# Attention and maxout feed-forward on one core: another written order of instructions and another list of masked tiles

## The chip, the cores and the metric

The kernel runs on one core of a Trainium2 chip. The core has a matrix engine (PE, with the loading of weights shown apart as PEld), a vector engine (DVE), a scalar engine (ACT), a general engine (POOL), and SP, which here only issues transfers to the 16 DMA engines. Every engine works through its own instructions in order and waits for others by semaphores. The metric is the device time of one execution in microseconds (us). Smaller is better.

## The reference

```python
scores = (1 / sqrt(64)) * q @ k.T                    # q, k, v: batch 8, heads 8, 576 rows, 64 columns
thresh = max(scores, axis=-1) - tau                  # tau = 0.02
scores = where(scores >= thresh, scores, -1e9)
attn = softmax(scores)                               # the sum gets + 1e-9
x = (attn @ v), heads side by side                   # 4608 x 512
h = maximum(maximum(x @ w1, x @ w2), x @ w3)         # 4608 x 768
out = h @ w_out                                      # 4608 x 512
```

The keep-or-drop decision is made against the row's largest score, so scores and softmax are done in 32-bit floats; the attention weights, v, x, h and the matrices of the feed-forward part are bf16.

## The kernel before

**Pieces.** The work is cut into pieces that the function `issue` emits one at a time. A *quad* is four heads of one batch (16 quads). A quad has 9 *chunks* of 128 query rows (four of head pair 0, one with the 64 rows that are left of each pair, four of pair 1). In a chunk each partition holds rows of two heads, so that a chunk has two *halves* (r = 0, 1), each a tile of 128 x 576 scores. Chunks run in the order of batches and quads; batch 7 alone (`SPLIT`) is cut into two parts, of 256 and of 320 rows.

**The order is written out by hand.** `ORDER` is one string of letters, and a loop at the end of the kernel calls `issue` on each. A letter takes the next piece of its kind, so the string sets only how the kinds interleave. Instructions of one engine keep the order of the string (`_Ordered` ties each to the one before it); between engines only data and buffers order them. The digit behind S, T, O, F is one of four PSUM slots (`bank`), and a slot must have been read out before the next piece takes it. All instructions of the pieces are recorded in `_Ordered.run`, line 90 of the kernel, so the profile tells them apart by tile, not by line.

| letter | engine | piece (tile in the profile) |
|---|---|---|
| S | PE | scores of one half (sc) |
| T | PE | transposes of q or k of a quad (tp); four per quad: q and k of r = 0, then of r = 1 |
| O | PE | attention weights times v (o), four per batch, four for each part of batch 7 |
| F, B | PE | first and second part of a feed-forward piece (ph: 18 per batch; po: the output). The 576-row pieces of ph and the po of two column blocks have both, the others F alone. The po of the last 64 rows of a batch ("ninth") is written among the pieces of the next |
| m | DVE | row maximum of a half, from PSUM; for a masked half it also writes the negated scores to z |
| e | ACT | masked: exp of z. Not masked: a Prelu with a very small negative slope, from PSUM to z |
| k | DVE | masked: drops what is below the threshold and sums (z<-z, SCALAR_TENSOR_TENSOR) |
| n | ACT | not masked: exp with the sum (z<-z, ACTIVATE and a read of the accumulator) |
| r | DVE | reciprocal of both sums of a chunk |
| p | POOL | multiplies one half by its reciprocal and writes bf16 (P), two per chunk |
| t | SP | DMA that transposes a chunk's P into ptq |
| a, c | ACT, DVE | q and k out of PSUM (qt, kt) |
| q | POOL | the other half of the partitions of q (qs) |
| x, w | ACT, DVE | x out of PSUM (xt) |
| h, v, u | ACT, DVE, ACT | ph to hm; the two maxima (hm, hT); po to the output tile (ob, obr) |
| l, g, o | SP | loads of q, k, v of a quad (eight: q's rest, k's rest, q, k, two of v, two of v's rest); load of a block of weights (stage, 512 KB, two buffers); store |
| y, z | POOL | cast of v (three per quad: vb, two of vr), of a block of weights (w, wo) |

An S of a half needs the quad's qt, qs and kt. An O needs nine t of its quad (four or five in batch 7's parts) and the y of it. The first F of a batch needs all four x or w of the batch, and the F of a block of weights its z. A g needs the z of two blocks before it.

**Two ways to the same half.** `MASKED` has one digit for each half, 288 in all, in the order of the S. A half with 1 goes m, e, k and costs DVE a pass over SBUF; its PSUM slot is free after m. A half with 0 goes m, e, n and costs ACT a second pass; its slot is free after e. Both give the same numbers up to rounding.

**In front of the string** (the prologue) the first quad is loaded, transposed and copied out, with some matmuls to warm PE up (`WARM`, `FILL`).

Of the kernel before, what the change touches and what calls it, by code (L numbers as in the profile page):

```python
# [21 lines left out]
FLAT = 2.0 ** -100  # L22

MASKED = """
101000100110000110011100001010010001100010001000101000010000100000100010
000011110101100001001001001001000001011100101011000110001010010000010011
001010011101100000101100100001001010000110011111000001000100000110000101
001001001101100000110001000100101000001100010011100101110110000001111111
"""


# [5 lines left out]
PBUFS = 6  # L37

ORDER = """
glllllS0lylS1mylyeS2zmlkS3lelmnlT0mS1aS2rmeqS0meqmeS3pnkT1pT0nrcaptemS0yeS1mgS2eympeS3mqtnT1S0mqnS2knrceprmS  # L40
1epkepeS3mnyS0rkptemnS2pmnlzmS3erremtpT0empS1eklpaS2kgnS0ptnmeprrmlS1epS3mleS2pmlS0eplmetpmeS1knS3tkernkS2pt
nmnprmtepmS1eqS0melpmT2ntrmT3pnrcpatekS3pekS2eqnrS1mtnqmS0pemepS3tmeqS2kepT1lnrcnprtmS0nT1pmS3epmgS2atpmeO1k
yermeO0knptrerT3wpnT2cS1aptmnS3pS2xmptS1emzS0emeS3zgmeS2lrmpnS0lmO1eplmeplknO3qlnrwleplkS1xqgS2ertmF3npF0meT
1pBrteBkyhS2cpnS3mpS1nvF2npmF0eqBmeqBrrvepS3tkhT2pS1nmS0lapmetS2pmeS3mzeF0mF1ezgBrnF2vpgnBktByeF0rvhpS3ntS2p
mF1npmBeBqrveT3zncT0F2taqvS3nBpmnS0tprhS1rmpeS3mtpS2emeyS0mteF1zmeF3kBelqBnvgF2pngT0vBnqlrS1cphS3lrmnS0plmO2
eplmeptS1ewpS3nmF0znmS2lBezkgO3etymyS1vegkF0ntF2nrrmpBxBpveS3phS0mtnF1prmeBprS2evptS3nmF0pnS1mplBermS3ztnS2v
nzS1meS0tmpeF3mperkS2petBmepmS0tkuF1ukelkT3elBkntrarmpS2uS3pmulS0eymtO1empnrO2kpewS3xpS1elmpF2lmF0eyqBrlkeT3
ytBhcF1pnT2vT3qlaBclnS0qvlS2nqtF3mnyF1meS0pBemBthrrF2kpeS3vnBpmF0nS1pveBrprS3mhtS2pmeS0pmeS1tpmF2emF3peBtkeT
0BvaF1onvqT2T0tBcqaS3nkqS0lhrmS2nlpmF1elpF3meBlkBelF0vntS2rvnBpS1mhplS3melF0mS2teBrmepS1rkpO3emnqO2tnrvpnwyS
0xlprS3emoF2pmoT1eyBpctS3evyF0nS1mtnS2pmBeympF1hkS3eyF2rekT0ptBamBnpS0veF3qtvS1urmnpS2mF3epketT0nkT1Bnrmparr  # L50
cpS2uS1pumtS0empS3emqoS1eF2mqlemqleS3kplnS0mBlepmlekT1teO3kunktO0urcpnrrwlS2nplS1xmpS3lmpS0eompS1eF2mtpeF3me
BkBetS0khF1nrmF2pnBvpBerrvS3phS0mtnpS1mF2peS3mtpeBmeF1yvF0etByknBvnS2tS3rhmpS1melpS0meF3lmF2elBkeBlvT1ntF0nv
T3BacS2ohS1rrmlpnF3lmF0peoBkpeBovnT2oS1qavS3tnprO2rmpmleqS0wtnT3pS1mepO2mteqkeqF0nS1cxBympnS3rS2hytmS1emF0pe
F3mpeBrkBpetF2vnF1pBnvS0thkS3nmF2BmeBveF0rrvpT1uS3kapS0nmS2F1pmtepmeS3rktepS0mnS2pmlBelrmeplS3kupS0lurmS2elp
F1mnoqmeS0qreS2lmpS3elmBpelmptekO0nketO2ukurrnwpT3T1xpcS0aF2ymyT3tpS1ceBqmS3thqF0meF2pknBtBnvF1nS3rtrvpeBmS0
phS2lmepS1lmyS3etF0meyF2mpeBkBetF1knF3vnBBrvhpS0nvT1pF2nmF3takBeS0rvplBmS1phlrS2remplF3mpleF0klBpeS1lvnS2lpm
nBtrO3mepvnptS2nwS1emF0mF3eBrkepS2hBrmS1nptvS0npT2meO3qmeycqlT0xT1yS2lacF3ntmyT0yeF1kqBatrBrevqF0hkS2pnoS3mF
1pmBteBpveS2qntS0vpnF3mprS1mlueS3pmoS0nqmtF2epmekT1oBerocpetrkS3npS1nmS0lpumS3uopmS1eT2mF0aokeorS3remplS2emt
pS1emBpeklqtkO3uqunO0rtmpewpT2xtS3cpeS0mnF2tF1meBknF3lkBhlBevF2nS0vnBmS1hrrS3pmeF0pmS2eBpmteF1pveF3kBlnS0vnl
S2rrBnmlpS1hrlmpF0eF3mtpeBkpBevtS2nF1pvnT0pBtmaS3hS0metF1rmepT2BrcepS3nvptT0S2nmyS1amS3lepmS0leO2mlelmeO1rkp  # L60
ewnT3pF0xcF2nykBnS1vnBrmS3phF0rrmepS2BynmqF1levF3qlBekpF0onvS2tBqmBhqrS1lepvT2S3lampF0lmS2peoBkpetF1vnS3prmu
S0ntqmS1eF2pmetpmeS3rkepS1tBmnpmelrS0keptS3muS1uymS0temT2yeF3pcntknT2BkelramtpS1nS2pmuS0leqrmO1tuqrkepO3nwep
mS1xpS2metF3pmS0eqBmeF1yhrkT2pBtecF3nS0vpnlS2rmpS1nlmBpnF0lveS2tmF3eBmeBkleF1klhF2lnrBvplS0nrrvptBnS3mphS1my
teS2mF3epmF0eBpeBtvpT1nrS2yvnlS3maF0omnqS1kBepF3temS2hpBrrmeS0ptveS1pmS3nptS2meO0pmeymnqlO3weokeoF1xkT0tT2S3
rcapBnmlF2pnS0vqtBerrmpS1hF3mqeT2BpncF0evptF2nkBpT1nvBlaS3ylS0hmoF1yqmT2eoBqrcnF0tpS3ervT2pBmaF1ytkqS2uvnS3q
mS1epF0mepmeS2kteT3BrnrcponmpS1uryS3umtS2emF0pepomeS1opnS2mtpeO3myektnO1wnkS2xrS3repmS1mpBekpteS2muS3purmF1e
pF0tmeBpkS3ntBhS2rnmpO1empO3xvS2xtnkS1eF3rmpF0emByepBveF1tkS2hS3mBmF0eF2rvepBBpvS1htkO3nmO0xkS2xeS3rmF0pF1me
pBeBtvS2F3vF0mF1kBeBkhF2nrvBpnBrvpS3hS0ptmS1pmeS2mtnF0mF3eBrnpBvnF1pS2vntS0rmpBmF3phoS2eS0omeF1tmBeBkO2vO0rv
pF3kpF1uketeF3kekBwrrkpBukxpuF2F0hptF1vF2pvF0hF1tvF2rvpF0hF1vpF2vF0thF1uvF2uvF0hoF3vF1vF2hoF0voO3oO1wovF2xF3
uoF0F1hF2vF0vF1hF2vF0vF1hF2vF0vF1hF2vF0vF1hF2vF0vF1hF2vBvF0uuooBF1uuuooo  # L70
"""


# [633 lines left out]
```

## Time and profile before

| | |
|---|---|
| median of 3 runs | 451.03 us (449.19 to 451.13) |
| profiled execution | 449.93 us; its span from first to last instruction 448.1 us |
| busy: PE, PEld | 427.0 us, 317.6 us |
| busy: DVE, ACT, POOL | 399.4, 392.4, 314.2 us |
| DMA | 87.44 MB in 212,773 packets, 195 GB/s over the span |
| granted TensorE clock, mean over the span | 0.988 |
| masked halves (k), others (n) | 109, 179 |

How to read it: busy is the time in which an engine worked on at least one instruction. PE's matmuls are pipelined and their ends are modelled, so that a busy PE need not be at its peak. In lines of groups, the number behind the bar is the group's busy time, then the mean time of one instruction in ns, then the idle time of the engine just before them and what ended it. Transfers issued by SP are listed under SPq; SP itself is never counted as busy. The page's 40 slices are 11.2 us each, their digits are tenths.

### The profile page before, as it was taken

How to read it: one execution, taken by the hardware profiler on the slowest of the kernel's cores; microseconds unless marked ns; L12 is line 12 of the kernel's file. 1: busy time of each engine (PE TensorE's matmuls, PEld its weight loads, DVE VectorE, ACT ScalarE, POOL GpSimd, SP SyncE). 2: the span in 40 equal slices, each digit the busy share in tenths (PEclk: the TensorE clock that was granted, in tenths of full speed). 3: DMA queues.
4: the chain of work that ended last, by engine and by line, in shares of the span. 5: the costliest groups of instructions: out<-in, count | busy, mean ns of one | idle time of the engine just before them, and what ended most of it. 6: DMA issues, size and time to landing. Idle time of an engine off the chain costs nothing.

```text
span 448.1 us, 14065 instructions
## 1 busy us (share of the span) xinstructions
PE 427.0 (95%) x5195; PEld 317.6 (71%) x5195; DVE 399.4 (89%) x1101; ACT 392.4 (88%) x793; POOL 314.2 (70%) x417
## 2 busy tenths in 40 slices
PE   7766889999999999999999999999999999999995
PEld 6524647767688768878687867868687787787762
DVE  3799999899999999999999999999999999999641
ACT  3899999999899999999999999999999999866422
POOL 3798889989785985587776785659777787534400
PEclk9898899999999999999999999999999999999999
DMA  8989999999999999999999997999998999546722
GB/s 235 266 195 188 234 238 190 249 244 220 250 192 193 187 236 209 207 215 179 227 175 205 228 217 176 217 230 205 197 195 203 204 156 194 108 78 132 130 95 107
DMA packets 212773, 87.44 MB, mean 195 GB/s; under 512 B 185824, under 2 KB 199648, under 8 KB 212704
## 3 DMA queue, kind: packets, MB, share of 16 engines
q1 hardware_dynamic: 212000, 85.69, 94.6%
q8 instruction: 41, 0.67, 0.6%
q10 hardware_dynamic: 704, 0.85, 0.6%
q14 instruction: 28, 0.23, 0.2%
HBM read 34.60 MB, written 9.44 MB: 98 GB/s over the span
## 4 chain that ended last, share of the span: by engine, by line
PE 77%; DVE 7%; ACT 5%; POOL 3%; DMA 3%; issue 2%; SPq 1%; DVEq 0%; POOLq 0%; ACTq 0%
PE ph L90 30%; PE sc L90 28%; PE po L90 10%; PE o L90 7%; ACT z L90 5%; DVE z L90 4%; PE tp L90 3%; DVE unused L90 2%; POOL P L90 2%; DMA qm<-in_q_dram 1%; DMA km<-in_k_dram 1%; SPq L90 1%; DVE hm L90 1%; DMA out_dram<-ob 1%; DVE kt L90 0%
## 5 line engine op out<-in xcount | busy, mean ns | idle before, releaser
L90 POOL TENSOR_SCALAR P<-z,rs 128x576 bf16<-128x576 f32 x288 | 228.8, 809 | 89.2 <-DVE rs L90 45.2
L90 PE MATMUL sc<-kt,qs 64*128 64x256 f32 (+2 forms) x640 | 180.5, 423 | 7.7 <-DVE z L90 2.0
L90 PE MATMUL sc<-kt,qt 64*128 64x320 f32 (+2 forms) x640 | 181.1, 433 | 4.0 <-DVE kt L90 1.2
L90 PE MATMUL ph<-xt,w 64*128 64x288 bf16 (+2 forms) x2160 | 165.5, 283 | 0.4 <-DVE hT L90 0.2
L90 PEld LDWEIGHTS <-w 64*128 64x128 bf16 (+1 forms) x2160 | 127.3, 94 | 29.8 <-issue 7.2
L90 ACT ACTIVATE z<-sc,nm 128x576 f32<-128x576 f32 x179 | 128.9, 740 | 10.8 <-DVE unused L90 9.5
L90 DVE TENSOR_SCALAR_CACHE_REDUCE unused<-sc 128x576 bf16<-128x576 f32 x179 | 130.5, 751 | 8.2 <-PE sc L90 7.3
L90 ACT ACTIVATE z<-z 128x576 f32<-128x576 f32 x179 | 120.8, 680 | 0.1
L90 PEld LDWEIGHTS sc<-kt,qs 64*128 64x128 f32 (+1 forms) x640 | 92.3, 179 | 30.9 <-ACT z L90 7.8
L90 PEld LDWEIGHTS sc<-kt,qt 64*128 64x128 f32 (+1 forms) x640 | 92.2, 178 | 20.0 <-ACT z L90 5.4
L90 DVE SCALAR_TENSOR_TENSOR z<-z 128x576 f32<-128x576 f32 x109 | 89.1, 832 | 0.2
L90 DVE TENSOR_SCALAR_CACHE_REDUCE z<-sc 128x576 f32<-128x576 f32 x109 | 80.5, 752 | 7.9 <-PE sc L90 4.6
L90 ACT ACTIVATE z<-z,nm 128x576 f32<-128x576 f32 x109 | 81.5, 772 | 2.6 <-DVE z L90 2.0
L90 POOL COPY qs<-qt 64x512 f32<-64x512 f32 (+1 forms) x63 | 45.0, 714 | 15.0 <-ACT qt L90 11.9
L90 PE MATMUL po<-wo,hT 64*128 64x512 bf16 (+1 forms) x480 | 54.0, 356 | 0.1
L90 DVE TENSOR_TENSOR hm<-ph,hm 128x576 bf16<-128x576 f32 (+2 forms) x54 | 37.1, 687 | 11.7 <-PE ph L90 11.3
L90 ACT ACTIVATE hm<-ph 128x576 bf16<-128x576 f32 (+2 forms) x54 | 32.1, 595 | 15.2 <-PE ph L90 13.7
L90 PEld LDWEIGHTS <-hT 64*128 64x128 bf16 (+1 forms) x480 | 29.3, 97 | 17.0 <-issue 3.1
L90 DVE TENSOR_TENSOR hT<-ph,hm 128x576 bf16<-128x576 f32 (+2 forms) x54 | 37.2, 688 | 3.8 <-PE ph L90 0.9
L90 PE MATMUL o<-ptq,vb 128*64 128x512 bf16 (+2 forms) x544 | 38.9, 282 | 0.2
L90 ACT ACTIVATION_READ_ACCUMULATOR z<-z 128x1 f32 x179 | 35.4, 198 | 0.0
L90 PEld LDWEIGHTS <-vb 128*64 128x64 bf16 x544 | 23.5, 111 | 14.4 <-issue 4.4
(33 smaller groups left out, 278.2 us busy)
## 6 DMA issues: line engine op xcount, KB each, us to landing
vm<-in_v_dram SPq DMA_DIRECT2D x32, 256.0 KB, 4.2
out_dram<-ob SPq DMA_DIRECT2D x31, 256.0 KB, 2.8
qm<-in_q_dram SPq DMA_DIRECT2D x15, 512.0 KB, 4.7
km<-in_k_dram SPq DMA_DIRECT2D x15, 512.0 KB, 5.1
stage<-in_moe_w_dram SPq DMA_DIRECT2D x9, 512.0 KB, 4.5
ptq<-P SPq DMA_TRANSPOSE x144, 4.2
stage<-in_moe_w_out_dram SPq DMA_DIRECT2D x3, 512.0 KB, 4.9
qm<-in_q_dram SPq DMA_DIRECT2D x16, 64.0 KB, 2.9
```

Source lines behind the costliest of these rows:

```text
L90: ins = fn(*a, **kw)
```

## The change

`ORDER` and `MASKED` are replaced. The new string is as long as the old (3,312 characters) and has the same number of every letter but two: k 105 instead of 109, n 183 instead of 179, in step with `MASKED`, whose rows have 21, 27, 25 and 32 ones instead of 23, 28, 27 and 31. Of the digits, slot 0 is taken 135 times (141), slot 1 142 (143), slot 2 149 (147), slot 3 144 (139). All engines get their letters in another sequence: the first letters that differ are the 1st of SP, the 3rd of DVE, the 4th of ACT and POOL, and the 10th of PE. The functions that make the pieces, the buffers and the prologue stay.

```diff
@@ -22,10 +22,10 @@
 FLAT = 2.0 ** -100
 
 MASKED = """
-101000100110000110011100001010010001100010001000101000010000100000100010
-000011110101100001001001001001000001011100101011000110001010010000010011
-001010011101100000101100100001001010000110011111000001000100000110000101
-001001001101100000110001000100101000001100010011100101110110000001111111
+001100101001000000011101001010000001100010001000101000011000100000100000
+000011111001100001001001001001000001011100101001000110001010010000010011
+000010011101100001001100100001001010001100010111000001000100000110000101
+001001001101100000110001000100100100001100100011100111010011010111110110
...
@@ -37,37 +37,37 @@
 PBUFS = 6
 
 ORDER = """
-glllllS0lylS1mylyeS2zmlkS3lelmnlT0mS1aS2rmeqS0meqmeS3pnkT1pT0nrcaptemS0yeS1mgS2eympeS3mqtnT1S0mqnS2knrceprmS
-1epkepeS3mnyS0rkptemnS2pmnlzmS3erremtpT0empS1eklpaS2kgnS0ptnmeprrmlS1epS3mleS2pmlS0eplmetpmeS1knS3tkernkS2pt
-nmnprmtepmS1eqS0melpmT2ntrmT3pnrcpatekS3pekS2eqnrS1mtnqmS0pemepS3tmeqS2kepT1lnrcnprtmS0nT1pmS3epmgS2atpmeO1k
-yermeO0knptrerT3wpnT2cS1aptmnS3pS2xmptS1emzS0emeS3zgmeS2lrmpnS0lmO1eplmeplknO3qlnrwleplkS1xqgS2ertmF3npF0meT
-1pBrteBkyhS2cpnS3mpS1nvF2npmF0eqBmeqBrrvepS3tkhT2pS1nmS0lapmetS2pmeS3mzeF0mF1ezgBrnF2vpgnBktByeF0rvhpS3ntS2p
-mF1npmBeBqrveT3zncT0F2taqvS3nBpmnS0tprhS1rmpeS3mtpS2emeyS0mteF1zmeF3kBelqBnvgF2pngT0vBnqlrS1cphS3lrmnS0plmO2
-eplmeptS1ewpS3nmF0znmS2lBezkgO3etymyS1vegkF0ntF2nrrmpBxBpveS3phS0mtnF1prmeBprS2evptS3nmF0pnS1mplBermS3ztnS2v
...
-pF0tmeBpkS3ntBhS2rnmpO1empO3xvS2xtnkS1eF3rmpF0emByepBveF1tkS2hS3mBmF0eF2rvepBBpvS1htkO3nmO0xkS2xeS3rmF0pF1me
-pBeBtvS2F3vF0mF1kBeBkhF2nrvBpnBrvpS3hS0ptmS1pmeS2mtnF0mF3eBrnpBvnF1pS2vntS0rmpBmF3phoS2eS0omeF1tmBeBkO2vO0rv
-pF3kpF1uketeF3kekBwrrkpBukxpuF2F0hptF1vF2pvF0hF1tvF2rvpF0hF1vpF2vF0thF1uvF2uvF0hoF3vF1vF2hoF0voO3oO1wovF2xF3
-uoF0F1hF2vF0vF1hF2vF0vF1hF2vF0vF1hF2vF0vF1hF2vF0vF1hF2vBvF0uuooBF1uuuooo
+lllS0llmlS1yelgS2ymylS3emgnlT0mleS1lakS2nlqermS3ylmeS0pmeS1kpS3elmS2nlzmelrmnT1pS0tcnperkT1pameS1zmteS3knpS0
+rnmpemS2permeqS1mnqT3meqktepS0ncS2ntrpmS3npretprmeS1pmnS0tpmS3npmS1etpmeS0rT2mnplkeT1akgeS2qmgepmteS3rkpeknt
+S0perrnmT2pncS3ptamepS1meqtrS2meyqnS3lmqeS0pmelpknT1lpS2nmeymeS3lrkepS0tcnT2rpnmS1tpnmaprrmS0eS2pmteS1pmT3ep
+ctepmeT3O0ykntnyS2etrykpnO1wnprmaS0xptrS3meS2zmeS1mzgeS0mlnS3pmleS1pmelO2qmelpkteO0nrnklpS3nlwgxprrmS2leS0pm
+eF3qtmT1eBqcF0eqkthBpnS2vS1nF3pmnF0pmBerBkepS2vhT1tnprmS0S3apmetS1zmeS2rmpeF3tmF0epBkepF1tnBvBznvS2ghS3rymnF
+0gmS1eplBrkepF2tnmF3BnpvBnqvT1S0hprrcT2S3pamS1eymzF2emBeqgkF0etyS3nS1vpnmtF2pBmezBveS3prgnS0mtS1phrmT3epO2me
+tzeF0wpnS1gcqS2nmBqnmO3zekepgS1xvlF2nS3mtnF0rrmpBeBlpveS1lphS2mntF3zmeBrpS0evS1lpnmF2lnpS3rmleBptmS1nzvS0nS3
+mtpnS2rpeF1rmepmtepS0mBepmtekF3ektekT2uBarklpukS0uqlS2urS1mlnS3pmleO0pmlepmelO2wtnkS1xrS0tepmF2myF3eBkepT1tB
...
+meF0opmnBtykBhpS1ervS2eptmO3pO0mxnS3txS2rmepF0empF1ekBtBevF3hkS2nS0mnBrmF1npF2vepBkBtS0hvO3emO2xkS1xerS3rpmF
+2mpF0eF1kpteBnBvpF3BvtBrhkpF2S0vS1prmBptmF3eF0pveBtBhS1vS2mS3mF0F1mBkBF2vhF3keBeO0vnO1kF2kxeBwurS1rvpS0mpS2F
+3mpetmpeS0eoF1mnketBknkBurrupoF2puF0hptF3uvF2pvF1hF0tvF3rvpF2hF1vopF0vF3thF2vF1vF0hoF3vF2ovF1hF0vF3vO2uoO1wF
+0xF3F2hF1vF3vF2hF1vF3vF2hF1vF3vF2hF1vF3vF2hF1vF3vF2hF1vBvF3uuooBF2uuuooo
 """
```

More of the change, by code (lines that the diff above doesn't have):

```diff
@@ L45 @@
-mF1npmBeBqrveT3zncT0F2taqvS3nBpmnS0tprhS1rmpeS3mtpS2emeyS0mteF1zmeF3kBelqBnvgF2pngT0vBnqlrS1cphS3lrmnS0plmO2
-eplmeptS1ewpS3nmF0znmS2lBezkgO3etymyS1vegkF0ntF2nrrmpBxBpveS3phS0mtnF1prmeBprS2evptS3nmF0pnS1mplBermS3ztnS2v
-nzS1meS0tmpeF3mperkS2petBmepmS0tkuF1ukelkT3elBkntrarmpS2uS3pmulS0eymtO1empnrO2kpewS3xpS1elmpF2lmF0eyqBrlkeT3
-ytBhcF1pnT2vT3qlaBclnS0qvlS2nqtF3mnyF1meS0pBemBthrrF2kpeS3vnBpmF0nS1pveBrprS3mhtS2pmeS0pmeS1tpmF2emF3peBtkeT
-0BvaF1onvqT2T0tBcqaS3nkqS0lhrmS2nlpmF1elpF3meBlkBelF0vntS2rvnBpS1mhplS3melF0mS2teBrmepS1rkpO3emnqO2tnrvpnwyS
@@ L50 @@
[L50 to L64, printed above, removed]
@@ L65 @@
-rcapBnmlF2pnS0vqtBerrmpS1hF3mqeT2BpncF0evptF2nkBpT1nvBlaS3ylS0hmoF1yqmT2eoBqrcnF0tpS3ervT2pBmaF1ytkqS2uvnS3q
-mS1epF0mepmeS2kteT3BrnrcponmpS1uryS3umtS2emF0pepomeS1opnS2mtpeO3myektnO1wnkS2xrS3repmS1mpBekpteS2muS3purmF1e
-pF0tmeBpkS3ntBhS2rnmpO1empO3xvS2xtnkS1eF3rmpF0emByepBveF1tkS2hS3mBmF0eF2rvepBBpvS1htkO3nmO0xkS2xeS3rmF0pF1me
-pBeBtvS2F3vF0mF1kBeBkhF2nrvBpnBrvpS3hS0ptmS1pmeS2mtnF0mF3eBrnpBvnF1pS2vntS0rmpBmF3phoS2eS0omeF1tmBeBkO2vO0rv
-pF3kpF1uketeF3kekBwrrkpBukxpuF2F0hptF1vF2pvF0hF1tvF2rvpF0hF1vpF2vF0thF1uvF2uvF0hoF3vF1vF2hoF0voO3oO1wovF2xF3
@@ new lines @@
+eF3qtmT1eBqcF0eqkthBpnS2vS1nF3pmnF0pmBerBkepS2vhT1tnprmS0S3apmetS1zmeS2rmpeF3tmF0epBkepF1tnBvBznvS2ghS3rymnF
+0gmS1eplBrkepF2tnmF3BnpvBnqvT1S0hprrcT2S3pamS1eymzF2emBeqgkF0etyS3nS1vpnmtF2pBmezBveS3prgnS0mtS1phrmT3epO2me
+tzeF0wpnS1gcqS2nmBqnmO3zekepgS1xvlF2nS3mtnF0rrmpBeBlpveS1lphS2mntF3zmeBrpS0evS1lpnmF2lnpS3rmleBptmS1nzvS0nS3
+mtpnS2rpeF1rmepmtepS0mBepmtekF3ektekT2uBarklpukS0uqlS2urS1mlnS3pmleO0pmlepmelO2wtnkS1xrS0tepmF2myF3eBkepT1tB
+hcF0nqvT2T1laByrcynS3qvS2nlqmF1tnpF0meS3pBelmBlhrrF2kpelS1vnBlprF3mnlS0pveBtprmS1hS2pmeS3tpmeS0pmF2emF1eBkeT
@@ new lines @@
+3BvatF0nvqT2T3BkqlaS1nrcS3phmtS2npmF0epF1mteBqkBeqF3lnvS2lnBrvplS0hmtpS1F3meS2mteBrmepS0vnpO1rekpnO3mtnpweS2
+yrrtxS1mF0yymT3epBcnS1pvS2nptF3meS0pmeBomT2hS1okeF0omF3ntBkaBervS1ponrF2vpemS0ptuS3mpeF2metknT1T3rknBparrceS
+0puS3mqtuS1mpeS2mpeS3lmF0peomepS1ketqT3S2ncBqnmlqnmlO3ekluktO1urnwperrS0pxS3mptnS2mS1pempS3etmF0peF2meBlkBel
+S1khoF3nrmlF0pnBtvpBerrvS2phlS1mnpS3tmF0peS2mpeBmeF3vF1eoBkntS0vnBS2rmhpS3mepS1mteyF2mF0eyBkteBnrvT3pF1aovT2
+ynBplrcS3hplS0mnyF2lmF1elBykepBlnvT3tS0aS2vnO3rrmtpnmpeS1weptS2mS0prmO3eqtmeqF1eqlT0S2xqcBnlpmS3hlpS0meF2ymF
@@ new lines @@
+1elBknlF3vnBokBetS2hvS0nrrF3mpF1mpeBkBpetF2vnprS0uvnT3ptmS2aS1pmeS0trmF3epmnpkeS2tS0ermpBnmopnkS1uS2rurompS0
+eF3ompelmpeS2lkpeS0lmS1elqBmelqmetkO2unktO0erwpurkpT1txT2cS3apF0nmtT1qS2ceBqmnS1yF3hmF2eyrBpeBvptnF0pS1vnBrm
+tpS3hS2pmeS0mtS1eF3meF2meBkBeF0knF1vnBBrvhpS3nvT0pF2akyF1tnBmyS0velByrmlS3phS2rlempF1lmyeF0pklBepS3tnvS2nBrm
+ptO1meprvepS2wnS3plmF0nF1rmepBlkeqS2lBhmtT3nyS0vnS2mqlO1emtpecT2xT0rS3pacF1eqmF2lnyBklqeT0BvlaS3khoS1qnmF0tF
+2pmeBrBopnvS3teprvF0pnrmS1puS2meS3prmS0epF1tmepmepT2ktBeqncT3tuS0kaS2urqmS3tnpmS1nF0pmemteS3repS1mS2lepmBely
@@ new lines @@
+kteS3kuO1rumplnmlpO0ewterpT2xS1cqnoS3mpF0nF2metBkeBkF1hlF3nvBlnrrS0pvlnBpmS2lhS1ymleF0mtS3epBmepF2vF1etkBnS0
+vnS3rmBnpS2rhmpF0emF1pteBkpBerF3vnS2ptvnT0pBramS1pthS0mepF3meqtT2rBecpS1nvylT0ynS2pmlS3amlS1eomS0elO2rmpeome
+plO3ketnwT1F0nctF2xkBnBrvpS1hrF3pmS0qBemqS2onvF1yeF0mBopkeF3tyBnS2vqhBrlrnmpT1S0vaptS2empF1S3mpelBkeplF0vntS
+2rumS1pnS0mtepF3rmepmetqS2kS0epBnmmteS1rkepS2lmuS0ulpmS1nlymT3yetF2cekeT3oBrknpamoS0npS3mnS1qtmuO0qurrmqelO2
+wpelkpelS0xS3meptF2mS1peBemytF0hrkT3pBecF2nS1vpnS3rymtBpnmS0epS1vlnF3mF2etBmeBkhF0lkeF3nBrvpS1nrvBpnS2mptS0h
@@ new lines @@
+mpeS3meF2tmF1eBkeBlrvnT0plS3ravlpS2nlmqF0nlS1mqeBtrrmpF2eS3phBlmepS0tvepS1mS2npS3mepO0meknO1meownT3orxkT2pS0
+tacF1nF2qrmeBtpS3evpBmS0tyhF1meT2yBcqoeF3rpkT2F0aptBnvBnS2pvS1hqtmF3nqT0meBrS1npvF2npmT3BactS1ervF3prmS0pueS
+2ompF3ekqelmT1ntS0qcnBpmekteS2S1urrmpF0uompekS3eptS2nmS1pnmlO3ermtpekO2pnwS1ykxtyS3emS2BomeyrmepS1rukpS2uoF3
+meF0opmnBtykBhpS1ervS2eptmO3pO0mxnS3txS2rmepF0empF1ekBtBevF3hkS2nS0mnBrmF1npF2vepBkBtS0hvO3emO2xkS1xerS3rpmF
+2mpF0eF1kpteBnBvpF3BvtBrhkpF2S0vS1prmBptmF3eF0pveBtBhS1vS2mS3mF0F1mBkBF2vhF3keBeO0vnO1kF2kxeBwurS1rvpS0mpS2F
```

## The prediction

> **What bounds the kernel now.** I read the page first, then busy time by stretch, then the waits, the timeline of the first 24 us, the chain, and the queue of SP. The profiled execution took 449.93 us: a span of 448.1 and 1.8 around it. The median of three runs is 451.03 (449.19 to 451.13), so the sum is made against 449.93 and then set on 451.03.
>
> The page, busy share and its 40 slices of 11.2 us:
>
> ```profile
> PE 427.0 (95%) x5195; PEld 317.6 (71%) x5195; DVE 399.4 (89%) x1101; ACT 392.4 (88%) x793; POOL 314.2 (70%) x417
> ...
> PE   7766889999999999999999999999999999999995
> ```
>
> PE has holes in its first six slices and nowhere else. By stretch (columns: PE, PEld, DVE, ACT, POOL busy, granted clock, DMA):
>
> ```profile
> 14.00:30.00 16.00, 12.29 (x98) 7.27 (x98) 14.35 (x43) 15.66 (x32) 12.85 (x18) 0.89 0.88 214
> 30.00:45.00 15.00, 10.06 (x86) 5.74 (x86) 14.45 (x46) 14.94 (x32) 13.22 (x17) 0.88 1.13 196
> 45.00:60.00 15.00, 12.77 (x124) 9.56 (x124) 14.56 (x40) 14.43 (x31) 13.77 (x17) 0.89 1.09 224
> 60.00:80.00 20.00, 19.22 (x231) 12.82 (x229) 19.12 (x56) 19.90 (x40) 18.35 (x24) 1.00 1.07 226
> 80.00:97.00 17.00, 16.93 (x219) 12.19 (x215) 16.03 (x42) 16.93 (x37) 16.23 (x22) 1.00 1.14 226
> 97.00:150.00 53.00, 52.86 (x680) 38.72 (x678) 50.16 (x140) 50.12 (x104) 42.00 (x56) 1.00 1.09 218
> 150.00:200.00 50.00, 49.89 (x643) 38.22 (x642) 48.70 (x134) 47.54 (x96) 35.88 (x49) 1.00 1.07 215
> 200.00:300.00 100.00, 99.95 (x1284) 76.54 (x1281) 94.84 (x262) 94.69 (x189) 71.06 (x95) 1.00 1.02 201
> 300.00:400.00 100.00, 100.00 (x1300) 78.48 (x1300) 94.14 (x260) 92.44 (x189) 71.85 (x99) 1.00 0.94 179
> ```
>
> Two regimes. From 14 to 97 ACT is busy 15.66 + 14.94 + 14.43 + 19.90 + 16.93 = 81.9 of 83 us, and PE, which has only scores to make until the first batch's softmax is through, 71.3: ACT sets the pace. From 97 to 400 PE is busy 302.7 of 303; ACT has 2.9 + 2.5 + 5.3 + 7.6 = 18.2 us to spare there. So the end moves by what the first stretch gains or loses and by any new hole in the second. One wait of the first stretch belongs to neither engine. The timeline at 12 to 24 us, and the chain:
>
> ```profile
> 13.43 0.53 PE L90 MATMUL tp<-identf,qm 64*128 64x64 f32 x10 [2.57 <-DMA qm<-in_q_dram]
> ...
> 13.99 0.70 ACT L90 ACTIVATE qt<-tp 128x640 f32<-128x640 f32 x1 [1.70 <-PE tp L90]
> ...
> 14.82 0.76 DVE L90 TENSOR_SCALAR_CACHE_REDUCE unused<-sc 128x576 bf16<-128x576 f32 x1 [1.88 <-PE sc L90]
> ```
>
> ```profile
> 7.90 5.39 DMA qm<-in_q_dram
> ```
>
> The second quad's q, issued at 7.90, lands at 13.29; PE, ACT and DVE all stand for it. What SP had issued before:
>
> ```profile
> 6.20 0.59 SPq L90 DMA_DIRECT2D stage<-in_moe_w_dram  x1
> 6.84 0.51 SPq L90 DMA_DIRECT2D qm<-in_q_dram  x1
> 7.39 0.47 SPq L90 DMA_DIRECT2D km<-in_k_dram  x1
> 7.90 0.47 SPq L90 DMA_DIRECT2D qm<-in_q_dram  x1
> ```
>
> **The change, part by part.** Counted by letter, the two texts hold the same pieces; only k goes from 109 to 105 and n from 179 to 183. Held against the trace, the old text is a time line: of the 2,425 letters of PE, ACT, DVE and POOL that I could lay on instructions, 96% start no more than 0.3 us before any that is written ahead of them. So places in the new text can be compared with places in the old.
>
> *PE's work.* Same letters, and the banks are used about equally often (135 to 149 times each, were 139 to 147): 0. An S takes 0.43 to 0.54 us to the next start, by its neighbour; S followed by S goes from 156 to 151 places, so at most 5 x 0.11 = 0.5 either way.
>
> *The masks.* Four fewer masked tiles: DVE loses four k, ACT gains four n.
>
> ```profile
> L90 ACT ACTIVATE z<-z 128x576 f32<-128x576 f32 x179 | 120.8, 680 | 0.1
> ...
> L90 DVE SCALAR_TENSOR_TENSOR z<-z 128x576 f32<-128x576 f32 x109 | 89.1, 832 | 0.2
> ```
>
> One n is 120.8/179 = 0.67 us, one k 89.1/109 = 0.82: ACT +2.7, DVE -3.3 in all. Behind 97 us the 18.2 us of ACT's room hide it; without that cover it would cost 2.7. In front of it the place decides: before the 75th S (which starts at 103.4 us in the trace) the new text has 49 n instead of 48 and 21 k instead of 23, with all other ACT letters (73 e, 8 a, 3 x, 6 h) and all PE letters equal. ACT paces here, so this costs one n: **+0.7** (bounds 0.7 to 1.3, since before the 59th S it is two n less one h, and before the 88th two n).
>
> *The start of SP's text.* Old: `glllll`; new: `lllllllg`. The 512 KB of `stage` go behind the second quad's q and k. That takes 0.64 us of issue (6.20 to 6.84) from in front of qm, and 0.52 MB from the transfers that it shares the engines with, at 0.32 to 0.38 MB/us (the slices of the DMA view from 8.5 us on) 1.4 to 1.6 us; the two overlap. The weights are not missed: z1 is written 1.5 us of PE work in, now 6.1, and the first F starts near 68 us. Also, ACT's letters ahead of the first a go from `een` to `eene`: 0.65 us of work falls into the 1.70 us hole. The gain on ACT is at least that 0.65 and at most the hole, 1.7. The landing term is nearer to the upper end, since qm then waits for nothing but its own quad: **-1.5**.
>
> *Loads moved.* Before the third quad's load is due nothing changes; for the fourth, q is issued 1.8 us of PE work ahead of its T where it was 4.4 (in ACT's letters 4.0 us, was 9.8). Loads issued near 42 and 50 us took 4.3 to 4.7 us from their place to landing. So PE may stand 0 to 0.7 us there, at about 45 us, while ACT has up to three written-out banks in front of it: 0, or 0.7 if it has none.
>
> *Transposing DMAs and products.* SP issues the 144 transposes in order with loads and stores, and an O waits for nine of them. The smallest rests between the landing and the O in the trace: 0.29 us at the third O (63.6), 0.34 at the seventh (118.2), 0.46 at the thirty-fifth (425.2), 1.6 at the fifth (94.6). In PE work, the last transpose is written ahead of these: third 2.8, now 3.3; thirty-fifth 3.1, now 3.9; fifth 5.8, now 4.3; seventh 6.3, now 5.0. The first two gain. The other two lie where SP runs late:
>
> ```profile
> 79.91 12.49 SPq L90 DMA_TRANSPOSE ptq<-P  x6
> ```
>
> From 79.9 SP issues without a pause, and the 27th transpose, written at 87.6, lands at 93.0: 5.4 us later; the 36th 6.6 us later. In the new text three more of them are out by 80 us (25 instead of 22), so the lag at these two should be some 3 x 1.3 us smaller. Bounds: 0 and 3.2 us (below); I take 0. The Trainium skill, Perfetto Trace Analysis, section What "DMA-bound" means, counts a kernel as DMA-bound where the issuing engine's track is solid with DMA slices; by that rule nothing gained on ACT would reach the end and the sum would be the rival's below, +2.4. The trace so far sides against it: every O found its tiles landed.
>
> *The end.* Four S move behind the thirty-third O, and the work that covers the last x is now the outp half of 1.3 us alone instead of ninth and outp (2.1 us); the last x is 0.43 us, so 1.3 still cover it. The stretch behind the last O is letter for letter the same. 0, bounds -0.3 and +1.0 (a wait for the last transpose).
>
> Sum: -1.5 + 0.7 = **-0.8**: 449.1 in an execution like the profiled one, 450.2 against the median.
>
> **Rivals.** (1) *SP comes late* (slower). Place: the fifth O. Its last transpose is written 4.3 us of PE work ahead (5.2 us at the rate at which 5.8 took 6.9), behind g9, which now waits for z7 (1.04 us), and with one more load (0.65) and one more g (0.5) ahead. If the lag stays 5.4, the tile lands 5.4 + 2.2 = 7.6 behind: PE stands 2.4 to 3.2. The seventh O adds up to 0.7 to 1.6 if the first stop has not let SP catch up. With the gain of 0.8: +1.6 to +3.9, say 454.0. It decides once the lag is over some 5.2 us. For it: SP's solid track, DMA share over 1.0. Against: three transposes moved ahead of 80 us. (2) *The fill gains all* (faster): the hole of 1.7 goes, with DVE 1.6 lighter by the 75th S half of ACT's 1.1 us of idleness goes, and PE's 0.85 us of idleness between 60 and 97 too: -1.7 + 0.7 - 0.6 - 0.85 = -2.5, 448.6. Against: e still waits on m across two engines. (3) *The load is not sooner*: qm is held by its own 512 KB and by k's; then -0.65 + 0.7 to 1.3, 451.0 to 451.7.
>
> **The numbers.** Forecast 0.38, rival 1 0.27, rival 2 0.22, rival 3 0.13. A measurement of this kernel can tell about 0.5% (2.3 us) from no change. Forecast and rival 3 lie within; of rival 2 nearly all passes -2.3 once its bounds are stretched by PE's 0.5; of rival 1 most passes +2.3. Faster 0.24, same 0.49, slower 0.27. The range leaves out the far ends of both: 447.2 to 454.6; the forecast's own is 449.0 to 451.6.
>
> **What would show it.** Right: the first tp<-qm matmul of the second quad starts near 12 us, ACT's gap in front of its qt is under 0.5, PE from 97 on is still busy 99.8%, O never waits on ptq, and ACT is busy some 395 us. Wrong: a PE wait named DMA ptq near 93 or 117 us (rival 1), tp still at 13.4 (rival 3), or PE holes from z or hm behind 100 us, which no row of before has.

## The result, and the profile after

The changed kernel took 446.46 us (median of 5, 446.20 to 447.21), the kernel before 451.03 in the same comparison (449.19 to 452.03): a ratio of 0.9911, interval 0.9883 to 0.9939. A second comparison of the same two gave 447.77 (7 runs, 446.23 to 449.69) and 0.9939, 0.9918 to 0.9961. Over all comparisons below the medians are 447.3 (13 runs) and 450.9 (97 runs): the change is worth 3.6 us, where I forecast 0.8. The profiled execution took 447.21 us with a span of 445.4 (449.93 and 448.1 before), a difference of 2.7. Two of the three kernels below that got idle matmuls also had longer runs at a lower mean clock (0.926 to 0.965), and their times and ratios are of the other runs alone.

The page after: PE has the same 5195 matmuls in 1.5 us less of busy time, although the half clock lasted longer in this fill (13.7 us, 10.2 before); ACT is 1.4 up, DVE 4.3 down.

```profile
PE 425.5 (96%) x5195; PEld 316.4 (71%) x5195; DVE 395.1 (89%) x1093; ACT 393.8 (88%) x801; POOL 314.9 (71%) x417
...
PE   7677799999999999999999999999999999999995
```

By stretch, the same stretches and columns as before (PE, PEld, DVE, ACT, POOL busy, granted clock, DMA share and GB/s):

```profile
14.00:30.00 16.00, 10.53 (x86) 5.94 (x84) 15.59 (x46) 15.38 (x34) 15.27 (x18) 0.88 1.03 244
30.00:45.00 15.00, 11.99 (x87) 9.10 (x88) 13.39 (x40) 14.17 (x29) 12.30 (x17) 0.73 1.10 213
45.00:60.00 15.00, 12.16 (x126) 7.76 (x122) 14.19 (x41) 14.89 (x33) 14.40 (x20) 0.95 1.06 212
...
97.00:150.00 53.00, 52.79 (x688) 39.78 (x684) 49.79 (x141) 50.77 (x104) 42.66 (x55) 1.00 1.12 227
150.00:200.00 50.00, 49.87 (x638) 37.16 (x636) 47.13 (x132) 48.70 (x100) 35.56 (x50) 1.00 0.96 205
200.00:300.00 100.00, 100.00 (x1307) 75.18 (x1305) 94.98 (x262) 96.22 (x196) 70.89 (x98) 1.00 0.98 204
300.00:400.00 100.00, 100.00 (x1286) 77.70 (x1285) 93.49 (x261) 91.51 (x185) 76.03 (x98) 1.00 0.93 181
```

The two regimes are still there. PE is busy 302.7 of 303 us from 97 on, as before, and the busy column alone would say that nothing happened there; the table of stretches below says otherwise. In the fill, the second quad's q, from the timeline and the chain:

```profile
11.55 0.53 PE L90 MATMUL tp<-identf,qm 64*128 64x64 f32 x10 [1.46 <-DMA qm<-in_q_dram]
12.12 0.70 ACT L90 ACTIVATE qt<-tp 128x640 f32<-128x640 f32 x1
...
7.33 4.08 DMA qm<-in_q_dram
```

It is issued 0.57 us sooner and takes 4.08 us instead of 5.39, lands 1.88 us sooner (11.41 for 13.29), and ACT's hole of 1.70 us is gone.

**Where the time went.** At the 661st letter and at the 2424th, both texts have issued the same pieces (83 S and 269 S), but for two and five k that are n in the new one. So the trace can be cut there: the time of PE's first instruction behind the 661st, from there to the first behind the 2424th, and from there to the end of PE's last matmul. Three executions of each text (us; the second and third are runs of their own below):

| execution | first S | to the 661st | 661st to 2424th | behind |
|---|---|---|---|---|
| before | 7.81 | 112.98 | 266.09 | 64.64 |
| before, second | 7.11 | 115.54 | 266.18 | 64.65 |
| before, third | 7.95 | 113.97 | 266.45 | 64.64 |
| after | 7.13 | 111.38 | 265.34 | 64.25 |
| after, second | 7.96 | 111.82 | 265.41 | 64.25 |
| after, third | 7.17 | 111.42 | 265.37 | 64.25 |

The means differ by 2.6 + 0.9 + 0.4 = 3.9 us, against 3.6 in the medians. Two things stand out. By these traces two thirds of the gain lie in the fill; but 1.3 us lie behind 111 us, in stretches that repeat within 0.4 us for the old text and 0.1 for the new. And all the scatter is in the fill: the old text's executions differ by 2.6 us there, and the profiled one was the quickest of its three. Three kernels below carry one of the two heads unaltered up to the 661st letter, and their traces make the fill's share less sure: 112.51 and 112.96 us with the old head, 114.11 with the new. Over all five and four executions the means are 113.6 and 112.2, and the fill gains 1.4 us instead of 2.6.

### The profile page after: what moved, and what is told of

Read it like the earlier page. It is cut to its first block, busy times and chain, and to the rows that moved or that the text cites. A ratio compares the mean times of both kernels' runs of the same rounds, so it can differ in the third digit from the quotient of the medians.

```text
span 445.4 us, 14085 instructions
## 1 busy us (share of the span) xinstructions
PE 425.5 (96%) x5195; PEld 316.4 (71%) x5195; DVE 395.1 (89%) x1093; ACT 393.8 (88%) x801; POOL 314.9 (71%) x417
## 4 chain that ended last, share of the span: by engine, by line
PE 82%; DVE 6%; ACT 5%; issue 3%; DMA 2%; POOL 1%; SPq 1%; DVEq 0%; POOLq 0%; ACTq 0%
PE ph L90 30%; PE sc L90 28%; PE po L90 11%; PE o L90 9%; ACT z L90 4%; PE tp L90 4%; DVE unused L90 2%; DVE z L90 2%; DMA km<-in_k_dram 1%; DMA qm<-in_q_dram 1%; POOL P L90 1%; SPq L90 1%; DVE hm L90 0%; DVE hT L90 0%; DVE kt L90 0%
## 5 line engine op out<-in xcount | busy, mean ns | idle before, releaser
L90 PEld LDWEIGHTS <-w 64*128 64x128 bf16 (+1 forms) x2160 | 124.8, 94 | 31.0 <-issue 5.1
L90 DVE TENSOR_SCALAR_CACHE_REDUCE unused<-sc 128x576 bf16<-128x576 f32 x183 | 133.3, 750 | 8.5 <-PE sc L90 7.5
L90 ACT ACTIVATE z<-sc,nm 128x576 f32<-128x576 f32 x183 | 131.2, 740 | 10.5 <-DVE unused L90 6.8
L90 ACT ACTIVATE z<-z 128x576 f32<-128x576 f32 x183 | 123.5, 681 | 0.1
L90 PEld LDWEIGHTS sc<-kt,qs 64*128 64x128 f32 (+1 forms) x640 | 94.3, 181 | 25.5 <-ACT z L90 7.0
L90 PEld LDWEIGHTS sc<-kt,qt 64*128 64x128 f32 (+1 forms) x640 | 94.5, 181 | 17.8 <-ACT z L90 9.2
L90 DVE SCALAR_TENSOR_TENSOR z<-z 128x576 f32<-128x576 f32 x105 | 85.2, 822 | 0.8 <-ACT z L90 0.8
L90 DVE TENSOR_SCALAR_CACHE_REDUCE z<-sc 128x576 f32<-128x576 f32 x105 | 77.7, 752 | 5.8 <-PE sc L90 3.5
L90 ACT ACTIVATE z<-z,nm 128x576 f32<-128x576 f32 x105 | 79.0, 773 | 3.5 <-DVE z L90 3.2
L90 PE MATMUL o<-ptq,vb 128*64 128x64 bf16 (+2 forms) x544 | 38.7, 282 | 0.0
```

What stands on the lines that cost most here:

```text
L90: ins = fn(*a, **kw)
```

## The experiments

**The two halves of the text.** One kernel takes the new text up to the 661st letter and the old behind it, the other the reverse.

```diff
-ORDER, MASKED: one text
+ORDER, MASKED: the first 661 letters of one text, the rest of the other
+   (slot digits of the rest renamed, a mask digit goes with the text that has the half's e)
```

> The new text and masks up to the 83rd S (about 110 us; to there both texts hold the same pieces), the old ones behind it. Theory A (the gain is made in the fill, where ACT paces, and PE then only carries it to the end): nearly the whole gain, some 447 us against 451 before. Theory B (most of it is made behind 110 us, in the order of PE's, DVE's and ACT's pieces there): the fill gives 1 to 2 us, 449.5. By the two profiled executions, where the same S is 1.6 to 1.8 us earlier at 100 to 120 us and 0.7 of that was there at the first S already, 449.3.

> The other half: the old text and masks up to the 83rd S, the new ones behind it. Theory A: no gain, 451. Theory B: most of the gain, 447 to 448.5. If the two parts add up, this one and the one with the new head together make up the 4.5 us between the medians.

New head: 449.36 us, ratio 0.9959 (0.9940 to 0.9978). New rest: 451.37, 1.0008 (0.9990 to 1.0026). Together 1.5 us of the 3.6: the halves don't add up, and neither theory holds as stated. The seam costs time. With the new rest behind the old head, 661st to 2424th takes 267.60 us, 2.2 more than in its own text (the old rest behind the new head: 267.14, 1.0 more), and these waits of PE between 105 and 215 us are in neither whole text:

```profile
PE tp L90 <- DMA qm<-in_q_dram: 0.5, 1, 0.5
PE sc L90 <- DVE hm L90: 0.5, 1, 0.5
```

They add up to 1.0 of the 2.2 us. So the new rest is 0.9 us quicker only behind what its own head leaves.

**The load of weights alone.** The first g, behind the second quad's loads in the old text; and in front of them in the new.

```diff
-glllllS0lylS1mylyeS2
+lllllS0lylgS1mylyeS2        (old text)
-lllS0llmlS1yelgS2
+glllS0llmlS1yelS2           (new text)
```

> The old text with one letter moved: the first load of weights goes behind the second quad's q and k (and two loads of v) on SP. If the early q is the gain of the fill, as my prediction has it: the second quad's first transpose starts 1.4 to 1.9 us sooner (near 11.8 us), ACT's hole of 1.7 us in front of qt shrinks, and the time falls by 0.7 to 1.7 us, 449.3 to 450.3. If the gain of the fill comes from the masks and the order of ACT's and DVE's letters, less than 0.5.

> The new text with the first load of weights put back in front of the second quad's q and k. If the early q is worth 1.5 us, some 448; if the new order of ACT's letters covers a later q (eene ahead of a), the 0.65 us that my lower bound left, 447; if it is worth nothing, 446.5.

Old text: 451.95 us, 1.0018 (1.0000 to 1.0035): no gain, rather a loss. New text: 449.40, 0.9964 (0.9948 to 0.9981): 2.1 of the 3.6 us gone. So the same move is worth 2 us in one text and nothing in the other. The one trace of the second run shows no hole at qt, but its first S is late (8.56), so the 2 us rest on its twelve times. What eats the gain in the old text stands in the next pair.

**Both moves at the second quad, made and undone.** With g, the order of e and a (ACT has one e more ahead of the first a in the new text).

```diff
-glllllS0lylS1 ... T0mS1aS2rmeqS0
+lllllS0lylgS1 ... T0mS1eaS2rmqS0      (old text)
-lllS0llmlS1yelgS2 ... T0mleS1lakS2
+glllS0llmlS1yelS2 ... T0mlS1laekS2    (new text)
```

> The old text with both of the new text's moves at the second quad: the load of weights behind its q and k, and the third e ahead of the first a. Theory F (the fill's gain is ACT's hole in front of the second quad's first qt): the hole of 1.7 to 2.5 us is gone in the trace and the median falls by 1.0 to 1.7, to 449.5 to 450. Theory G (the fill's gain is spread over the later letters, and the hole only absorbs a late start): within 0.5 of the kernel before.

> The new text with both moves taken back: the load of weights in front of the second quad's q and k, and the fourth e behind the first a. Theory F: the hole in front of qt returns with 1.5 to 2.5 us, and the median is 1.0 to 2 us over that of the changed kernel (447.4 over its twelve runs so far), at 448.5 to 449.5. Theory G: under 0.7 over it.

New text without both: 449.04 us, 0.9963 (0.9937 to 0.9990), 1.7 over the changed kernel, and the hole is back with 2.81 us: theory F, in the new text.

```profile
14.16 0.70 ACT L90 ACTIVATE qt<-tp 128x640 f32<-128x640 f32 x1 [2.81 <-PE tp L90]
```

In this trace the two later stretches keep their 265.37 and 64.25 us. So of the 3.6 us the two moves are worth some 1.7, the later stretches 1.3, and some 0.6 are left for everything else in the fill (each to about 1 us, by the intervals of the times). Old text with both: 452.17, 1.0038 (1.0014 to 1.0063). The second quad's transpose starts at 11.59 and the hole is gone, and yet it is slower. The timeline of POOL, then of ACT, says why:

```profile
16.66 1.04 POOL L90 CAST w<-stage 128x1024 bf16<-128x1024 f32 x1 [4.60 <-DMA stage<-in_moe_w_dram]
17.77 1.47 POOL L90 COPY qs<-qt 64x640 f32<-64x640 f32 x2
19.34 1.46 POOL L90 TENSOR_SCALAR P<-z,rs 128x576 bf16<-128x576 f32 x2
```

```profile
20.12 0.74 ACT L90 ACTIVATE z<-sc,nm 128x576 f32<-128x576 f32 x1 [1.47 <-POOL P L90]
...
26.06 0.74 ACT L90 ACTIVATE z<-sc,nm 128x576 f32<-128x576 f32 x1 [1.25 <-POOL P L90]
```

In the old text POOL's cast z stands early. With its load late, POOL stands there for 4.60 us, qs and P queue behind it, the z buffers come free late, and ACT loses 1.47 + 1.25 where it won 1.70. In the new text the z is written 4.6 us of PE work later, and POOL comes to that cast (at 17.40) without an idle gap. By these traces the move of g pays only together with the move of z, which I had noted and not priced; an old text with its z moved too was not run.

**The end alone.**

```diff
-ORDER, MASKED: old text
+ORDER, MASKED: old text to the 2424th letter, new text behind
```

> The old text and masks up to the 269th S (some 379 us; to there both texts hold the same pieces), the new ones behind. In the traces so far the pieces behind that place take 64.25 us in the new text and 64.64 in the old, most of it one stall of 0.32 us of PE in front of a piece of the feed-forward part (waiting for hT) that the new text doesn't have. If that is the order's doing, the trace shows 64.25 here and the end is 0.4 us sooner, 450.6 to 450.8 in the median; if the state that the new text hands over makes it, 64.64.

450.97 us, 1.0003 (0.9976 to 1.0030); behind the 2424th letter 64.78 us. Neither expected figure: the new end keeps its 64.25 only behind the new text from the 661st letter on. The old end, in turn, takes 64.33 in the kernel with the new head. So the stretch hangs on what is handed over to it, and not on its order alone. In the old text's trace the stall in question is this one, in the new there is none:

```profile
419.40 0.81 PE L90 MATMUL ph<-xt,w 128*128 128x256 bf16 x6 [0.15 <-DVE hT L90]
```

```profile
415.24 3.00 PE L90 MATMUL ph<-xt,w 128*128 128x256 bf16 x26
```

**The changed kernel again,** for scatter and a second trace (no edit).

> The changed kernel unaltered, for more times and a second trace. By the trace of one execution the change is worth 0.68 at the first S (prologue, not changed), 0.92 from there to 111 us, 0.75 to 377 us and 0.39 behind, 2.7 in all; the medians say 4.6. If the rest is scatter of the start and of the stretches of half clock in the fill, the median of more runs comes to 447 to 448.5 and the last two numbers return within 0.1, while the first two change by a microsecond or more. If the order itself is worth it all, the median stays at 446.5.

447.77 us; the trace is the second row above. The last two parts return within 0.1, the scatter is in the first.

**Half clock.** In the fill the granted clock falls to 0.5 for stretches of 3 to 10 us. In the changed kernel's first execution they lie at 26 to 33 and 40 to 47 us, in its second at 22 to 25 and 49 to 53, in its third there is none. The Trainium skill, TensorE: Matmul & The Clock Gate, Part 1, says that the clock is halved after an idle window of some 3.4 us and that the windows run free of the kernel; places that change from execution to execution agree with free windows. A window without any work is not what these traces show: between 8 and 111 us no gap of PE is over 1.7 us in the three executions. In all traces of this document together there are 27 half-clock stretches between 10 and 60 us, and each follows 3.4 us in which PE was busy 0.24 to 0.59 of the time. Three kernels put matmuls behind the first 52 S, to keep PE busier:

```diff
+        if 2 * number[...] + r < 52:
+            tensor.transpose(ps[:, 0:128], identf, identf)      (the first two)
+            tensor.matmul(ps[:, 0:32], identf, identf[:, 0:32], ...)      (the third)
         return ps[:, first:first + S]
```

> The changed kernel with one idle 128 x 128 transpose behind each of the first 52 S, into a part of its slot that nobody reads, so that PE stands less in the fill. It adds 52 x 0.15 = 7.8 us of PE work (more at half clock) where PE has some 10 us of idle time. If the half-clock stretches come of PE's low load and cost time, they get fewer and shorter (mean clock up from 0.985 towards 1.0), the runs lie closer together, and the median is 445 to 447. If they cost nothing (ACT paces), the same or up to 3 us slower, by the added work.

> The same transposes in the kernel before. If the new text's gain over 2.7 us is that its fill meets the half clock more rarely or at better places, the difference between this and the changed kernel with the same transposes is near 2 (0.9 + 0.75 + 0.39), and this one is 448 to 450. If the gain lies in the order alone, the difference stays at 4.5.

> The changed kernel with a matmul of 32 columns instead of the 128 x 128 transpose behind each of the first 52 S, some 0.1 us where that was 0.33. The large one drove the clock to 1.0 and the runs together (452.9 to 453.95), but cost 5.4 us. If PE's load alone sets the half clock, the mean clock rises to 0.993 or more and the runs spread less; 445.5 to 447 if the half clock costs more than the 52 matmuls, 448 to 450 if PE's extra work lies on the path.

453.03 us (452.89 to 453.95; 1.0058, 1.0037 to 1.0079), 457.49 in four runs (1.0146, 1.0122 to 1.0170) and 456.71 in three (1.0124, 1.0073 to 1.0175). All three are slower than without the added matmuls. The edits were mis-sized. The transpose takes twice what I reckoned, and the small matmul was emitted as two matmuls with a weight load each, more PE time than the transpose:

```profile
L90 PE MATMUL sc<-identf 128*128 128x128 f32 x51 | 16.7, 328 | 0.0
```

```profile
L90 PE MATMUL sc<-identf 128*128 128x32 f32 x102 | 20.8, 286 | 0.0
```

What they do show: with PE loaded the half clock leaves the fill (1.0 from 0 to 72 us in the traces of the changed kernel with either matmul), and the six runs of the first lie within 1.1 us. They don't show what the half clock costs, but they do show that the new text does not gain by meeting it less: with the same transposes, and the full clock from 12 us on in both traces, the two texts differ by 4.5 us (457.49 and 453.03), no less than without. What the half clock costs, the unaltered text shows better:

```profile
14.00:30.00 16.00, 9.32 (x82) 4.72 (x82) 15.41 (x46) 15.03 (x33) 14.46 (x17) 1.00 1.10 248
30.00:45.00 15.00, 10.87 (x96) 5.81 (x96) 14.02 (x43) 14.92 (x31) 13.70 (x18) 1.00 1.02 199
45.00:60.00 15.00, 11.44 (x120) 6.71 (x120) 13.43 (x39) 14.50 (x33) 14.48 (x19) 1.00 1.13 227
```

This is its third execution, at full clock throughout: 111.42 us to the 661st letter, against 111.38 with 13.7 us at half clock up to 47. There it is free: ACT, which paces, has the same idle time in both (3.5 and 3.6 us, below). In the new head with the old rest, which has the same text up to there, the clock is halved from 49 to 59 us, over the first products, and ACT stands for the copy of x:

```profile
45.00:60.00 15.00, 11.71 (x86) 7.81 (x88) 10.81 (x32) 13.21 (x29) 11.81 (x18) 0.66 1.09 208
```

```profile
61.18 0.65 ACT L90 ACTIVATE xt<-o 128x576 bf16<-128x576 f32 x1 [2.16 <-PE o L90]
```

The 661st letter is then at 114.11, 2.3 to 2.7 us later than in the three executions of the changed kernel, where ACT stands no more than 0.19 us for this x. So a stretch of half clock costs nothing or some 2 us by where it falls; the 2 us rest on this execution and on one more below.

**Two n turned into k** (the 32nd and the 71st half, in the fill of the changed kernel).

```diff
-MASKED: half 32: 0, half 71: 0     ORDER: epS0tcnT2r ... lphS2mntF3
+MASKED: half 32: 1, half 71: 1     ORDER: epS0tckT2r ... lphS2mktF3
```

> The changed kernel with two more masked halves in the fill (the 32nd and the 71st: k on DVE in the place of n on ACT). In the traces ACT's work from the prologue to the 661st letter is 99.8 us in the new text and 98.9 in the old, by two n more. If ACT still sets the pace there, 2 x 0.66 us of it go and the median is 0.7 to 1.3 us under that of the changed kernel (447.4): 446.1 to 446.7. If DVE (busy 90 to 97% of the same stretch) or the handing over between the engines sets it, the same or up to 1.6 slower.

451.60 us, 1.0010 (0.9990 to 1.0030): 4.3 us slower than the changed kernel. In the trace ACT's work to the 661st letter falls by 0.9 us (99.8 to 98.9; I had counted 1.3 for the two n), and its idle time rises from 3.2 to 3.6 in the three traces of the changed kernel to 8.7. Its waits between 9 and 113 us:

```profile
ACT z L90 <- DVE unused L90: 4.3, 9, 0.8
ACT xt L90 <- PE o L90: 2.3, 1, 2.3
ACT z L90 <- DVE rs L90: 1.0, 1, 1.0
```

In the second execution of the changed kernel the first of these is 2.4 us (6 times) and the last is absent. The 2.3 us at x belong to a half clock at 50 to 60 us in this execution; the other 3 us of idle time are waits on DVE, which had the two k added. The half clock is not all of the loss: the six runs at a mean clock of 0.984 or more lie at 450.0 to 451.5, their median 3.3 us over that of the changed kernel's runs at such a clock. A tile moved from the engine that paces is no gain when the other is nearly as full (DVE was busy 78.6 of 83 us from 14 to 97, ACT 80.7).

**More traces of both** (no edit, one execution each).

> The kernel before unaltered, for a second trace. The first has 112.98 us to the 661st letter, 266.09 from there to the 2424th and 64.64 behind. The last two should return within 0.1. If the traced execution was one of the quicker ones of its kind (its median says some 114 for the first part), this one lies at 113 to 115, by a later start or a stretch of half clock where PE is needed.

> As the second trace: 113 to 115 to the 661st letter if the old text's fill is usually slower than the first trace shows; 112.5 to 113 if that trace is typical, and then the medians differ for another reason.

> The changed kernel for a third trace: 111.4 to 111.9 us to the 661st letter as in the first two, then 265.4 and 64.25.

452.61, 451.33 and 447.31 us; their rows are in the table. Both executions of the old text have a slower fill than the first trace; the two other kernels with its head (112.51 and 112.96) don't. The second execution shows the hole at twice the size:

```profile
13.96 0.80 PE L90 MATMUL tp<-identf,qm 64*128 64x64 f32 x10 [3.93 <-DMA qm<-in_q_dram]
14.79 0.70 ACT L90 ACTIVATE qt<-tp 128x640 f32<-128x640 f32 x1 [3.33 <-PE tp L90]
```

ACT's account from its last instruction of the prologue to the 661st letter, us of work and of idle time: before 98.9 + 4.9, 98.8 + 7.9, 99.1 + 5.6; after 99.8 + 3.6, 99.8 + 3.2, 100.0 + 3.5.

## Why the prediction was wrong

The forecast was -0.8, the medians say -3.6. By the undone moves and the stretches, the 2.8 us that are missing come from four terms: the early q some 0.2, the masks and the rest of the fill's order some 1.3, PE's work 0.9, the end 0.4. The first two are good to about 1 us only.

*The early q* (-1.5, bounds 0.65 to 1.7). The mechanism is right in the new text: transpose at 11.55 (11.51 and 11.41 in the other two), no hole, and undoing the two moves costs 1.7 us, undoing g alone 2.1. The size was taken from one execution. The hole is 1.70, 3.33, 1.73, 2.46 and 2.20 us in the five executions with the old head. The transpose behind it starts at 13.39 to 13.96 us in all five, whenever PE and ACT began; a quick start only makes the hole longer (first S at 7.11, hole 3.33; at 7.95, 1.73). So the size of one hole was no bound. The transpose is 2.0 us sooner in the mean, and that is the steadier figure.

*The masks* (+0.7). This step failed. ACT's extra work is there: 0.9 us more to the 661st letter. But I let it count in full against the fill, with the k that it replaces at no price, because ACT paces. The new order of the fill without the two moves is not slower than the old one but some 0.6 us quicker, and turning two n back into k cost 4.3 us. With these two k more, ACT's waits on DVE grew by some 3 us, so DVE's list holds ACT up as well. How much of this is the masks and how much the order was not tried apart.

*PE's work* (0, +-0.5) and *the end* (0, -0.3 to +1.0). These failed too: -0.9 and -0.4, both outside their bounds. I read "busy 302.7 of 303" as no room, but starts of pieces can draw closer within busy time. From the 661st to the 2424th letter, in the mean of three executions, the 22 transposes of eight matmuls take 6.62 us in the old text and 6.02 in the new to the next piece's start, the 180 half pieces of ph 90.9 and 90.4, the 22 products 29.2 and 28.9, the 168 S of four matmuls 88.6 and 89.1. I had priced S against S alone. Whether it is the neighbours or short waits is not shown.

*From the profiled execution to the median* (+1.1). The old median lies 1.0 us over its profiled execution, the new one 0.1. So 0.9 of the 3.6 us are not in the pair of profiled executions, and which ones were profiled is luck. The hole does not explain it: the times scatter as much without it (standard deviation 1.0 us for either text), and the old head came to the 661st letter soonest (112.51) with a hole of 2.46. With the 1.1 left out the forecast is 449.1, still 1.8 too high. The stated range began at 447.2; the first median (446.46) lies under it, the second (447.77) and that of all runs (447.3) just inside.

*Loads moved* (0). Right in effect, by the argument given: in the second and the third execution PE does stand for the fourth quad's q (0.95 us to 49.76 and 1.17 us to 49.85), for longer than the 0.7 that I allowed, and ACT, with work written out in front of it, does not stand for it.

*Transposing DMAs and products* (0, rival 1 at 3.2). Right, but by a small margin, and at the place that rival 1 named: the fifth O, 1.56 us behind its last tile before, follows it by 0.27, 0.40 and -0.15 us (recorded landings) in the three executions after, the smallest of all, and PE has no wait on ptq. In the old text's second and third execution the third and the seventh O lie as close (-0.14 to -0.31); in the new text these have 0.58 us or more. By the rule of the Trainium skill, Perfetto Trace Analysis, What "DMA-bound" means, a gain on ACT would not have reached the end; it did. But SP's track is no longer solid there: a transpose ends at 85.76, the next transfer is issued at 87.49. So the new text is no full test of that rule.

*The signs.* Transpose near 12, gap under 0.5, PE busy 99.8% behind 97, no O waiting, ACT at 393.8 busy for 395: all five came true, and the median of the first comparison was still 3.7 us lower than I said. They could not tell the forecast from a larger gain. Rival 2 (448.6) came nearest, by the hole; PE's idle time from 60 to 97 fell by 0.3 us of its 0.85, and its account ended at 97 us.

*Open.* The plain difference of the fill is 2.6 us by three traces each, with 1.8 of it on ACT's account; 0.2 is an earlier start, and 0.6 lies between ACT's last letter and PE's next piece (an S in the old text, an F in the new) and was not followed. What the new masks alone are worth was not tried apart: the list decides when a slot comes free, and each text takes its slots by its own list.

## What to carry to other kernels

Before a hole is priced, look at it in several executions: a hole in front of a transfer takes up the scatter of what runs ahead of it, and the start of the work behind it says more than its size. When a transfer is moved back, look for its consumer on the consumer's own queue; here the stall moved to what was queued behind that consumer. Extra work on the engine that paces is not a plain loss when it takes work from an engine that is nearly as full. In this hand-written order a part kept its gain only behind its own head: test a piece by undoing it in the new order, and not only by adding it to the old one.

## What was not expected of the hardware

Half clock was free while another engine paced (13.7 us of it cost nothing up to 47 us) and cost some 2 us over the first products. It came without any long gap of PE, behind 3.4 us in which PE was busy less than 0.6 of the time. A 32-bit matmul of 32 columns against a full identity came out as two matmuls with a weight load each, 286 ns apiece, where a 128 x 128 transpose took 328 ns.
